# Clustered attention and a feed-forward block: seven block products for eight, and the feed-forward work moved behind the attention

## The chip, the cores and the metric

The kernel runs on one core of a Trainium2 chip. The metric is the device time of one execution in microseconds. The kernel before takes 1087.33 us (median of three runs, 1086.96 to 1087.64).

The core has a matrix engine (TensorE, PE in the profile, with PEld for its weight loads), VectorE (DVE), ScalarE (ACT), GpSimd (POOL) and SyncE (SP), which issues the transfers here.

## What is computed

Attention in which a query sees only the keys of its own cluster, then a feed-forward block without bias:

```python
# q, k, v: (4, 8, 768, 64); centroids: (8, 16, 64)
q_assign = argmax(q_n @ c_n.T);  k_assign = argmax(k_n @ c_n.T)   # of 16 clusters, per head
scores = q @ k.T / sqrt(64), where q_assign == k_assign, else -1e9
attn_out = softmax(scores) @ v                                    # (4, 8, 768, 64)
x = attn_out as (4 * 768, 512)                                    # tokens x (heads * 64)
h = x @ w_in                                                      # (3072, 2048)
g = h * sigmoid(1.702 * h)
out = g @ w_out                                                   # (3072, 512)
```

All matmuls are done in float32. The weights arrive as float64 and are turned into float32 on the chip, early in the run.

## The kernel before

The names: a *pair* is two heads of a batch (16 pairs). A *unit* is one tile of 128 keys against half of the queries (384) of both heads of a pair. Six units make a *group* g. A batch has 8 groups, first four for its first half of queries, then four for the second. The main loop goes through 96 *steps* t of two units each, 24 steps to a batch.

```python
ps_s: 2 score buffers of two PSUM banks each;  ps_o: 1 bank;  ps_m: 3 banks  # bank()

def scores(u):      # TensorE: k^T q of both heads into a score buffer      (L384)
def exps(u):        # ScalarE: exp, in place in the score buffer            (L409)
def mask(u):        # VectorE: A = (code of query == code of key) * exp     (L420)
                    # GpSimd: sum of A over the units of the group          (L430)
def values(u):      # TensorE: o += v^T A                                   (L441)
def normalise(g):
    # TensorE: column sums of `sum` by a matmul with ones, into bank()      (L453)
    rec = recs[g] = short()
    nc.vector.reciprocal(out=rec, in_=ps[:, 0:HALF])                      # (L456)
    nc.vector.tensor_tensor(out=x, in0=x, in1=rec, op=ALU.mult)           # (L458)
    if g % HP == HP - 1:                  # four pairs done: half of a batch
        ffn.extend(ffn_chunks(g // HP))
def check(g):       # is rec within limits?
    nc.scalar.activation(out=rec, in_=rec, func=AF.Copy, accum_out=...)   # (L468)
    nc.scalar.activation(out=rec, in_=rec, func=AF.Relu, ..., accum_out=...)  # (L470)

# ffn_chunks(half of a batch): 16 chunks `first`, then 12 chunks `second`
def first(f):       # 4 matmuls of 384 columns into bank()                  (L487)
    nc.scalar.activation(out=g, in_=ps, func=AF.Tanh, scale=0.851)        # (L492)
    nc.vector.scalar_tensor_tensor(g = (g + 1) * ps)                      # (L494)
def second(n, part):  # 4 matmuls of 512 columns; one bank for 4 chunks     (L504)
    # after the last part: ScalarE halves it to y (L510), transfer to out

# prep of a pair, seven parts: turns i = 0..3 (L262, ScalarE copy L267),
# near (L276), assign (VectorE L293 to L316), spread (transfers)
t = b * TB + (-20, -8, -2, 1)[hp] + i       # step of part i of pair hp of batch b

for t in range(NT + 2):
    scores, exps, mask of units 2t, 2t + 1
    values of the two units before
    normalise(g), if a group ended two steps ago       # from mid-batch 0 on; earlier
    prep parts of this step                            # steps do prep first
    if recs: check(*recs)
    owed += rate; as many chunks of ffn as are owed    # rate = 28 / 11.5 = 2.43
# ... some cuts: the unpacking of weights in batch 0 (`round_next`)
while ffn: ffn.popleft()()                  # what is left at the end
```

So each half of a batch is fed forward while the next half's attention runs.

Of the kernel before, what the change touches and what calls it, by code (L numbers as in the profile page):

```python
# [8 lines left out]
FP32 = mybir.dt.float32  # L9
BF16 = mybir.dt.bfloat16  # L10
I32 = mybir.dt.int32
U32 = mybir.dt.uint32
U8 = mybir.dt.uint8
AF = mybir.ActivationFunctionType
ALU = mybir.AluOpType
AX = mybir.AxisListType
# [22 lines left out]
def fast(  # L39
# [18 lines left out]

    nc = tc.nc

    B, H, S, D = q.shape
    NC = centroids.shape[1]
    DM, DF = moe_w_in.shape
# [8 lines left out]
    SCALE = D ** -0.5  # L74
    LIMIT = float(2 ** 20)
    FAR = float(2 ** 120)
    assert D == 64 and NC == 16 and H * NC == P and NJ == 6 and DM == H * D

    PS = bass.MemoryType.PSUM
    NPB = HP + 1  # L80
    const = ctx.enter_context(tc.tile_pool(name="const", bufs=1))
    inp = ctx.enter_context(tc.tile_pool(name="inp", bufs=3))
    pairs = ctx.enter_context(tc.tile_pool(name="pairs", bufs=NPB))
    wp = ctx.enter_context(tc.tile_pool(name="wp", bufs=3))
    asg = ctx.enter_context(tc.tile_pool(name="asg", bufs=2))
    tmp = ctx.enter_context(tc.tile_pool(name="tmp", bufs=3))
    ap = ctx.enter_context(tc.tile_pool(name="ap", bufs=4))
    xp = ctx.enter_context(tc.tile_pool(name="xp", bufs=HP + 2))
    gp = ctx.enter_context(tc.tile_pool(name="gp", bufs=NF))
    yp = ctx.enter_context(tc.tile_pool(name="yp", bufs=2))  # L90
    dram = ctx.enter_context(tc.tile_pool(
        name="dram", bufs=2, space=bass.MemoryType.DRAM))
    ps_s = ctx.enter_context(tc.tile_pool(name="ps_s", bufs=2, space=PS))
    ps_o = ctx.enter_context(tc.tile_pool(name="ps_o", bufs=1, space=PS))
    ps_m = ctx.enter_context(tc.tile_pool(name="ps_m", bufs=3, space=PS))
    ctx.enter_context(tc.manual_schedule())

    def bank():
        return ps_m.tile([P, 512], FP32, name="m")
# [54 lines left out]
    def split_w(i):  # L154

        hi = w_raw[i][:, :, 1]
        w = w_chunks[i][0]
        e = wp.tile([P, WN], I32, name="e")
        nc.vector.tensor_scalar(out=e, in0=hi, scalar1=EXP, scalar2=None,  # L159
                                op0=ALU.bitwise_and)  # L160
        nc.vector.tensor_scalar(out=w.bitcast(I32), in0=hi, scalar1=0xFFFFF,
                                scalar2=None, op0=ALU.bitwise_and)
        nc.scalar.activation(out=e, in_=e, func=AF.Relu, scale=8.0,  # L163
                             bias=low[:, 0:1])
        nc.scalar.activation(out=w, in_=w.bitcast(I32), func=AF.Copy,
                             scale=2.0 ** -20, bias=1.0)
        w_pow[i] = e
# [14 lines left out]
    def round_next():  # L182
        i = w_done[0]
        if i < NW:
            load_w(i + 2)
            split_w(i)
        if 0 < i <= NW:
            join_w(i - 1)
        w_done[0] += 1
# [25 lines left out]
    rank = const.tile([P, NC], BF16, name="rank")  # L215
    nc.vector.tensor_copy(out=rank, in_=rank_f)

    hot = const.tile([P, NJ * 4, 32], BF16, name="hot")
    nc.vector.memset(hot, 0.0)
    sums = const.tile([P, 2, 2 * NPAIR], FP32, name="sums")  # L220

# [226 lines left out]
    def normalise(g):  # L448

        sm = sum_of.pop(g)  # L450
        ps = bank()
        for a in range(2):
            nc.tensor.matmul(out=ps[a * D:(a + 1) * D, 0:HALF], lhsT=ones,  # L453
                             rhs=sm[:, a, :], start=True, stop=True)
        rec = recs[g] = short()
        nc.vector.reciprocal(out=rec, in_=ps[:, 0:HALF])  # L456
        x = xT_of[g] = O_of.pop(g)
        nc.vector.tensor_tensor(out=x, in0=x, in1=rec, op=ALU.mult)  # L458
        if g % HP == HP - 1:
            ffn.extend(ffn_chunks(g // HP))  # L460

    recs = {}

# [8 lines left out]
                             accum_out=sums[:, 1, g:g + 1])  # L472


    ffn = deque()

    def ffn_chunks(bh):
        b, h = divmod(bh, 2)
        xT = [xT_of.pop(bh * HP + c) for c in range(NCH)]
        hs, ys = {}, {}  # L480

        def first(f):

            round_to((f * P // WN + 1) * NCH)
            ps = bank()
            for c in range(NCH):
                nc.tensor.matmul(out=ps[:, 0:HALF],  # L487
                                 lhsT=w_in[:, c, f * P:(f + 1) * P],
                                 rhs=xT[c], start=(c == 0),
                                 stop=(c == NCH - 1))  # L490
            g = hs[f] = gp.tile([P, HALF], FP32, name="g")
            nc.scalar.activation(out=g, in_=ps[:, 0:HALF], func=AF.Tanh,  # L492
                                 scale=0.851)
            nc.vector.scalar_tensor_tensor(out=g, in0=g, scalar=1.0,  # L494
                                           in1=ps[:, 0:HALF], op0=ALU.add,
                                           op1=ALU.mult)

        def second(n, part):
            round_to(NW // 2 + 4 * (part + 1))
            if part == 0:  # L500
                ys[n] = bank()
            ps = ys[n]
            for f in range(4 * part, 4 * part + 4):
                nc.tensor.matmul(out=ps[:, 0:DM],  # L504
                                 lhsT=hs[f][:, n * P:(n + 1) * P],
                                 rhs=w_out[:, f, :],
                                 start=(f == 0), stop=(f == NF - 1))
            if part == NF // 4 - 1:
                y = yp.tile([P, DM], FP32, name="y")
                nc.scalar.mul(y, ps[:, 0:DM], 0.5)  # L510
                nc.sync.dma_start(
                    out=out[b * S:(b + 1) * S, :].rearrange(
                        "(p j) n -> p j n", j=NJ)[:, h * NH + n, :], in_=y)

        return ([lambda f=f: first(f) for f in range(NF)]
                + [lambda n=n, part=part: second(n, part)
                   for n in range(NH) for part in range(NF // 4)])

# [6 lines left out]
    for p in range(1, NPAIR):  # L527
        b, hp = divmod(p, HP)
        for i in range(2 if p == 1 else 0, len(PREP)):
            if p == 1:  # L530
                t = (i - 2) // 2
            elif b == 0:
                t = (hp - 2) * TG + 1 + i // 2
            else:
                t = b * TB + (-20, -8, -2, 1)[hp] + i
            prep_at.setdefault(t, []).append((p, i))
    loads = deque((p, w) for p in range(NPAIR) for w in range(2))
    for _ in range(3):
# [15 lines left out]
    for t in range(NT + 2):  # L554
        us = range(2 * t, 2 * t + 2) if t < NT else ()
        for u in us:
            scores(u)
        if t == 0:
            prep(0, 6)
        for u in us:  # L560
            part(u)
        for u in us:
            exps(u)
        second = t >= TB // 2
        if second:
            round_next()
        for u in us:
            mask(u)
        work = sorted(prep_at.get(t, ()), key=lambda w: PREP[w[1]] != prep_near)
        while work and PREP[work[0][1]] == prep_near:  # L570
            prep(*work.pop(0))
        if 1 <= t <= NT:
            for u in range(2 * t - 2, 2 * t):
                values(u)
        owed = owed + rate if ffn else 0.0
        g = (t - 2) // TG if t >= 2 and (t - 2) % TG == TG - 1 else None
        if g is not None and second:
            normalise(g)
        for p, i in work:
            prep(p, i)  # L580
        if g is not None and not second:
            normalise(g)
        if recs:
            check(*recs)
        if second or t and t % 4 != 3:
            round_next()
        while owed >= 1 and ffn:
            ffn.popleft()()
            owed -= 1
        if second and t % 2:  # L590
            round_next()


    ok = const.tile([P, 2, 2 * NPAIR], FP32, name="ok")
    nc.vector.tensor_scalar(out=ok, in0=sums, scalar1=LIMIT, scalar2=None,
                            op0=ALU.is_le)
    ok1 = const.tile([P, 1], FP32, name="ok1")
    nc.vector.tensor_reduce(out=ok1, in_=ok, axis=AX.XY, op=ALU.min)
    for _ in range(NF // 2):
        ffn.popleft()()  # L600
    ps = bank()
    nc.tensor.transpose(out=ps[0:1, 0:P], in_=ok1, identity=ident)
    okt = const.tile([1, 1], FP32, name="okt")
    nc.vector.tensor_reduce(out=okt, in_=ps[0:1, 0:P], axis=AX.X, op=ALU.min)
    bad = const.tile([1, 1], I32, name="bad")
    nc.vector.tensor_scalar(out=bad, in0=okt, scalar1=-1.0, scalar2=1.0,
                            op0=ALU.mult, op1=ALU.add)
    while ffn:
        ffn.popleft()()
        if len(ffn) == 4:  # L610
            is_bad = nc.values_load(bad[0:1, 0:1], min_val=0, max_val=1)
    return is_bad


@with_exitstack
def general(
# [436 lines left out]
```

## Time and profile before

| engine | busy us | share |
|---|---|---|
| PE (TensorE) | 1049.0 | 96% |
| DVE (VectorE) | 490.8 | 45% |
| ACT (ScalarE) | 354.8 | 33% |
| POOL (GpSimd) | 296.9 | 27% |

The same by stretches of the run, in us of busy time:

| stretch | PE | DVE | ACT | POOL | granted clock |
|---|---|---|---|---|---|
| 0 to 100 | 80.14 | 71.81 | 53.78 | 46.54 | 0.95 |
| 100 to 190 | 80.53 | 85.75 | 50.21 | 26.03 | 0.94 |
| 190 to 280 | 88.93 | 33.09 | 29.05 | 23.34 | 1.00 |
| 280 to 400 | 120.00 | 50.52 | 35.03 | 34.55 | 1.00 |
| 880 to 1000 | 120.00 | 47.20 | 32.55 | 34.37 | 1.00 |
| 1000 to 1087 | 81.40 | 9.53 | 9.65 | 0.00 | 0.99 |

How to read it: [...] A line of a group gives the source line, the engine and operation, the tile written and those read, the shapes and the count. After the first bar stand the busy time and the mean duration of one in ns, and after the second the idle time of the engine just before, with what ended it. In the timeline, a row is the start in us, the time covered in us, and the instructions merged into it, and in brackets the idle time before. The granted clock is the share of full speed that TensorE was given. Matmuls overlap each other, so their durations add up to more than the time they occupy.

### The profile page before, as it was taken

The numbers are of one execution on the slowest core, as the hardware profiler recorded it, in microseconds if no ns is written. First come the engines' busy times: TensorE is split into PE (matmuls) and PEld (weight loads), VectorE is DVE, ScalarE is ACT, GpSimd is POOL, SyncE is SP. The second block draws the span as 40 slices with busy tenths as digits, with TensorE's granted clock in tenths as the row PEclk, the third lists the DMA queues.
The fourth block names the chain that finished last, engine by engine and source line by source line (L and its number), as shares of the span: only waits on it lengthen the run. The fifth ranks groups of instructions, "written<-read, shape, count | busy, mean of one in ns | idle before, by whom it ended". The sixth has DMA issues, their size and how long they took to land. (4 is left out here: it accounts for less than half of the span.)

```text
span 1087.3 us, 10456 instructions
## 1 busy us (share of the span) xinstructions
PE 1049.0 (96%) x3982; PEld 492.6 (45%) x3982; DVE 490.8 (45%) x744; ACT 354.8 (33%) x665; POOL 296.9 (27%) x168
## 2 busy tenths in 40 slices
PE   7878799999999999999999999999999999999997
PEld 3423344445544455444454445444554445444543
DVE  3889999225442344424453164423552344431200
ACT  3755555223422333223432233223332133311100
POOL 2644223213232333123231142222332333230000
PEclk9998899999999999999999999999999999999999
DMA  7623443110100010002100000010000000000000
GB/s 199 165 81 116 131 133 111 46 49 17 49 23 27 10 30 15 31 25 54 51 23 17 15 20 15 15 48 32 8 7 12 10 10 1 1 10 20 1 11 22
DMA packets 64813, 45.13 MB, mean 42 GB/s; under 512 B 51953, under 2 KB 57585, under 8 KB 64753
## 3 DMA queue, kind: packets, MB, share of 16 engines
q1 hardware_dynamic: 64608, 44.33, 14.3%
q8 instruction: 33, 0.54, 0.2%
q14 instruction: 28, 0.22, 0.1%
q10 hardware_dynamic: 144, 0.03, 0.0%
HBM read 38.04 MB, written 6.31 MB: 41 GB/s over the span
## 5 line engine op out<-in xcount | busy, mean ns | idle before, releaser
L430 POOL TENSOR_TENSOR sum<-sum,A 128x768 f32<-128x768 f32 x128 | 235.5, 1840 | 461.3 <-DVE A L420 364.1
L487 PE MATMUL m<-x,w_in 128*128 128x384 f32 x1024 | 347.1, 494 | 9.7 <-ACT T L267 4.4
L504 PE MATMUL m<-w_out,g 128*128 128x512 f32 x768 | 337.8, 594 | 0.7 <-ACT short L282 0.7
L420 DVE SCALAR_TENSOR_TENSOR A<-qb,code,s 128x384 f32<-128x384 uint8 x288 | 157.6, 609 | 274.6 <-ACT s L409 251.9
L487 PEld LDWEIGHTS m<-x,w_in 128*128 128x128 f32 x1024 | 192.2, 192 | 149.1 <-issue 16.3
L504 PEld LDWEIGHTS m<-w_out,g 128*128 128x128 f32 x768 | 143.3, 190 | 175.6 <-issue 171.5
L494 DVE SCALAR_TENSOR_TENSOR g<-g,m 128x384 f32<-128x384 f32 x128 | 70.0, 553 | 220.4 <-ACT g L492 220.3
L384 PE MATMUL s<-T,T 64*128 64x384 f32 x768 | 152.9, 517 | 9.7 <-ACT A L409 9.6
L409 ACT ACTIVATE s<-s 128x768 f32<-128x768 f32 x144 | 107.9, 792 | 136.0 <-PE s L384 136.0
L441 PE MATMUL o<-A,inv 128*64 128x384 f32 x768 | 146.3, 502 | 0.0
L492 ACT ACTIVATE g<-m 128x384 f32<-128x384 f32 x128 | 61.7, 487 | 196.4 <-PE m L487 196.3
L430 POOL TENSOR_TENSOR sum<-A 128x768 f32<-128x768 f32 x32 | 60.0, 1876 | 215.6 <-DVE A L420 179.5
L384 PEld LDWEIGHTS s<-T,T 64*128 64x128 f32 x768 | 66.6, 189 | 94.6 <-issue 52.2
L456 DVE RECIPROCAL short<-m 128x384 f32<-128x384 f32 x32 | 81.6, 2551 | 25.8 <-PE m L453 25.8
L441 PEld LDWEIGHTS o<-A,inv 128*64 128x64 f32 x768 | 46.8, 137 | 84.8 <-issue 84.1
L510 ACT ACTIVATE y<-m 128x512 f32<-128x512 f32 x24 | 14.3, 595 | 155.8 <-PE m L504 142.7
L468 ACT ACTIVATE short<-short 128x384 f32<-128x384 f32 x32 | 16.7, 523 | 111.2 <-DVE x L458 111.2
L409 ACT ACTIVATE A<-s 128x768 f32<-128x768 f32 x48 | 36.1, 804 | 22.0 <-PE s L398 22.0
L267 ACT COPY T<-m 128x384 f32<-128x384 f32 x64 | 29.7, 480 | 37.2 <-PE m L262 37.1
L262 PE MATMUL m<-ident,in 128*128 128x128 f32 x192 | 33.9, 298 | 3.1 <-ACT T L267 1.7
L163 ACT ACTIVATE e<-e,low 128x512 int32<-128x512 int32 x32 | 23.1, 722 | 28.8 <-DVE e L159 28.8
L262 PEld LDWEIGHTS m<-ident,in 128*128 128x128 f32 x192 | 21.5, 146 | 22.4 <-issue 11.9
(68 smaller groups left out, 373.5 us busy)
## 6 DMA issues: line engine op xcount, KB each, us to landing
raw<-in_moe_w_in_dram SPq DMA_DIRECT2D x16, 512.0 KB
raw<-in_moe_w_out_dram SPq DMA_DIRECT2D x16, 512.0 KB
in<-in_q_dram SPq DMA_DIRECT2D x32, 192.0 KB
in<-in_k_dram SPq DMA_DIRECT2D x32, 192.0 KB
inv<-in_v_dram SPq DMA_DIRECT2D x16, 384.0 KB
out_dram<-y SPq DMA_DIRECT2D x24, 256.0 KB
qb<-line SPq DMA_DIRECT2D x12, 192.0 KB
line<-row SPq DMA_DIRECT2D x12, 1.5 KB
```

What stands on the lines that cost most here:

```text
L262: nc.tensor.transpose(out=ps[:, n * P:(n + 1) * P], in_=qk_in[p, w][:, h * NH + n].rearrange("p a d -> p (a d)"), identity=ident)
L267: nc.scalar.copy(dst, ps[:, 0:HALF])
L384: nc.tensor.matmul(out=ps[:, a, 0:HALF], lhsT=T[p, 1][rows, kt * P:(kt + 1) * P], rhs=T[p, 0][rows, h * HALF:(h + 1) * HALF], start=True, ...
L409: nc.scalar.activation(out=A_of[u] if p < HP else s, in_=s, func=AF.Exp, scale=SCALE)
L420: nc.vector.scalar_tensor_tensor(out=A_of[u][:, a, :], in0=qcode[p][:, a, h * HALF:(h + 1) * HALF], scalar=code[p][:, kt % NH, 1, kt // NH ...
L430: nc.gpsimd.tensor_tensor(out=sum_of[g], in0=A_of[u - 1] if kt == 1 else sum_of[g], in1=A, op=ALU.add)
L441: nc.tensor.matmul(out=o_of[g][a * D:(a + 1) * D, 0:HALF], lhsT=v_in[p][:, a, kt, :], rhs=A[:, a, :], start=(kt == 0), stop=(kt == NJ - 1))
L456: nc.vector.reciprocal(out=rec, in_=ps[:, 0:HALF])
L487: nc.tensor.matmul(out=ps[:, 0:HALF], lhsT=w_in[:, c, f * P:(f + 1) * P], rhs=xT[c], start=(c == 0), stop=(c == NCH - 1))
L492: nc.scalar.activation(out=g, in_=ps[:, 0:HALF], func=AF.Tanh, scale=0.851)
L494: nc.vector.scalar_tensor_tensor(out=g, in0=g, scalar=1.0, in1=ps[:, 0:HALF], op0=ALU.add, op1=ALU.mult)
L504: nc.tensor.matmul(out=ps[:, 0:DM], lhsT=hs[f][:, n * P:(n + 1) * P], rhs=w_out[:, f, :], start=(f == 0), stop=(f == NF - 1))
```

## The change

The first layer of the feed-forward block is h = w_in^T x. Take w_in as 2 x 2 blocks (halves of the 2048 outputs by halves of the 512 inputs), and x as 2 x 2 blocks (halves of the inputs by the two halves of a batch's tokens). This product of blocks takes eight block products. There is a scheme with seven products and fifteen block additions or subtractions (Winograd's form of Strassen's), and the change uses it for batches 1, 2 and 3. For this it needs both halves of a batch's x at once, sums of weight blocks (made once) and sums of x blocks (per batch), and room for them in SBUF, which is there only when the attention's buffers are free. So these three batches are fed forward behind all attention.

The attention of batches 1 to 3 would then have no other matmuls beside it. Batch 0's second half is kept for that: it is cut into 48 small chunks (token tiles of 128: two f of the first layer, or two f of the second), of which 0.62 are done in a step, and the last eight are kept for the moment when the sums are made. Batch 0's first half is fed forward as before, during its second half's attention.

For room, pairs have four buffers, not five, and the preparation of a batch's first pair starts 8 steps ahead, not 20. The three banks of `ps_m` stay. Behind the attention, the score banks and the `o` bank become five banks `ps_b` for the seven products.

The core of the diff (cuts marked ...):

```diff
-    NPB = HP + 1
+    NPB = HP
-    xp = ctx.enter_context(tc.tile_pool(name="xp", bufs=HP + 2))
-    gp = ctx.enter_context(tc.tile_pool(name="gp", bufs=NF))
+    xp = ctx.enter_context(tc.tile_pool(name="xp", bufs=NX))        # NX = 26
+    gp = ctx.enter_context(tc.tile_pool(name="gp", bufs=NF // 4))   # of 512 columns
 ...
+    def ffn_tiles():                       # batch 0, second half
+        def first2(n, i):
+            ps = bank()
+            for f in (2 * i, 2 * i + 1):
+                for c in range(NCH):
+                    nc.tensor.matmul(out=ps[:, f % 2 * P:(f % 2 + 1) * P],
+                                     lhsT=w_in[:, c, f * P:(f + 1) * P],
+                                     rhs=xT[c][:, n * P:(n + 1) * P], ...)
+            ...                             # tanh and gelu of 256 columns
+        def second2(n, i): ...              # two matmuls of 512 columns
 ...
-                t = b * TB + (-20, -8, -2, 1)[hp] + i
+                t = b * TB + (-8, -5, -2, 1)[hp] + i
 ...
-        owed = owed + rate if ffn else 0.0
+        todo = half_ffn or (ffn if len(ffn) > NF // 2 else ())
+        owed += (rate if half_ffn else 0.62) if todo else -owed
 ...
+    ps_b = ctx.enter_context(tc.tile_pool(name="ps_b", bufs=5, space=PS))
+    def sums_w(lo, hi): ...                 # VectorE: 8 sums of weight blocks
+    def sums_x(b): ...                      # VectorE: 8 sums of x blocks
+    def seven(f, X, T, gs):
+        def product(a, x):
+            ps = ps_b.tile([P, 512], FP32, name="b")
+            for c in range(2):
+                nc.tensor.matmul(out=ps[:, 0:HALF], lhsT=a(c), rhs=x(c), ...)
+            return ps[:, 0:HALF]
+        p = product(lambda c: A(0, 0, c, *r), lambda c: X[0, 0, c])
+        nc.scalar.copy(g1[:, 0], p)
+        p = product(lambda c: Sa(2, c, *r), lambda c: T[2, c])
+        add(g2[:, 1], p, g1[:, 0])          # VectorE
+        ...                                 # five more products, six more adds
+        for g in (g2, g1):
+            gelu(g, th.tile([P, 2, HALF], FP32, name="th"), g)
+
+    sums_w(0, 2 * P)
+    XT = sums_x(1)
+    sums_w(2 * P, FB * P)
+    while ffn:
+        ffn.popleft()()                     # the eight chunks left
 ...
+    for b in range(1, B):
+        for f in range(FB):                 # FB = 8
+            seven(f, *XT, gs)
+        for h in range(2):
+            for n in range(NH):
+                if (h, n) == (0, 1) and b < B - 1:
+                    XT = sums_x(b + 1)
+                ...
+                for f in range(NF):
+                    second(2 * b + h, n, f, gs[f][:, h, n * P:(n + 1) * P], ps)
```

More of the change, by code (lines that the diff above doesn't have):

```diff
@@ L76, in fast @@
     FAR = float(2 ** 120)
+    NX = 6 * HP + 2
     assert D == 64 and NC == 16 and H * NC == P and NJ == 6 and DM == H * D
     PS = bass.MemoryType.PSUM
-    NPB = HP + 1
+    NPB = HP
     const = ctx.enter_context(tc.tile_pool(name="const", bufs=1))
[L82 to L87, printed above, removed]
-    xp = ctx.enter_context(tc.tile_pool(name="xp", bufs=HP + 2))
-    gp = ctx.enter_context(tc.tile_pool(name="gp", bufs=NF))
[L90 to L94, printed above, removed]
+    xp = ctx.enter_context(tc.tile_pool(name="xp", bufs=NX))
+    gp = ctx.enter_context(tc.tile_pool(name="gp", bufs=NF // 4))
+    yp = ctx.enter_context(tc.tile_pool(name="yp", bufs=1))
     ps_m = ctx.enter_context(tc.tile_pool(name="ps_m", bufs=3, space=PS))
     ctx.enter_context(tc.manual_schedule())
+    att = ExitStack()
+    inp = att.enter_context(tc.tile_pool(name="inp", bufs=3))
+    pairs = att.enter_context(tc.tile_pool(name="pairs", bufs=NPB))
+    wp = att.enter_context(tc.tile_pool(name="wp", bufs=3))
+    asg = att.enter_context(tc.tile_pool(name="asg", bufs=2))
+    tmp = att.enter_context(tc.tile_pool(name="tmp", bufs=3))
+    ap = att.enter_context(tc.tile_pool(name="ap", bufs=4))
+    hp1 = att.enter_context(tc.tile_pool(name="hp1", bufs=1))
+    dram = att.enter_context(tc.tile_pool(
+        name="dram", bufs=2, space=bass.MemoryType.DRAM))
+    ps_s = att.enter_context(tc.tile_pool(name="ps_s", bufs=2, space=PS))
+    ps_o = att.enter_context(tc.tile_pool(name="ps_o", bufs=1, space=PS))
     def bank():
@@ L157, in split_w @@
         w = w_chunks[i][0]
-        e = wp.tile([P, WN], I32, name="e")
+        e = wp.tile([P, WN], I32, name="e", bufs=2)
         nc.vector.tensor_scalar(out=e, in0=hi, scalar1=EXP, scalar2=None,
@@ L216, in fast @@
     nc.vector.tensor_copy(out=rank, in_=rank_f)
-    hot = const.tile([P, NJ * 4, 32], BF16, name="hot")
+    hot = hp1.tile([P, NJ * 4, 32], BF16, name="hot")
     nc.vector.memset(hot, 0.0)
@@ L458, in normalise @@
         nc.vector.tensor_tensor(out=x, in0=x, in1=rec, op=ALU.mult)
-        if g % HP == HP - 1:
-            ffn.extend(ffn_chunks(g // HP))
+        if g % HP == HP - 1 and g < 2 * HP:
+            (half_ffn, ffn)[g // HP].extend((ffn_half, ffn_tiles)[g // HP]())
     recs = {}
@@ L472, in check, with gelu, second, ffn_half @@
                              accum_out=sums[:, 1, g:g + 1])
[L475 to L480, printed above, removed]
+    def gelu(g, t, h):
+        nc.scalar.activation(out=t, in_=h, func=AF.Tanh, scale=0.851)
+        nc.vector.scalar_tensor_tensor(out=g, in0=t, scalar=1.0, in1=h,
+                                       op0=ALU.add, op1=ALU.mult)
+    def second(bh, n, f, g, ps):
+        nc.tensor.matmul(out=ps[:, 0:DM], lhsT=g, rhs=w_out[:, f, :],
+                         start=(f == 0), stop=(f == NF - 1))
+        if f == NF - 1:
+            b, h = divmod(bh, 2)
+            y = yp.tile([P, DM], FP32, name="y")
+            nc.scalar.mul(y, ps[:, 0:DM], 0.5)
+            nc.sync.dma_start(
+                out=out[b * S:(b + 1) * S, :].rearrange(
+                    "(p j) n -> p j n", j=NJ)[:, h * NH + n, :], in_=y)
+    half_ffn, ffn = deque(), deque()
+    def ffn_half():
+        xT = [xT_of.pop(c) for c in range(NCH)]
+        gs, ys = {}, {}
         def first(f):
@@ L490, in first, with second3 @@
                                  stop=(c == NCH - 1))
[L491 to L498, printed above, removed]
+            g = gs[f] = (xp.tile([P, HALF], FP32, name="x") if f % 4 else
+                         gp.tile([P, 4 * P], FP32, name="g")[:, 0:HALF])
+            gelu(g, g, ps[:, 0:HALF])
+        def second3(n, part):
             round_to(NW // 2 + 4 * (part + 1))
@@ L501, in second, with second2 @@
                 ys[n] = bank()
-            ps = ys[n]
             for f in range(4 * part, 4 * part + 4):
[L504 to L513, printed above, removed]
-        return ([lambda f=f: first(f) for f in range(NF)]
-                + [lambda n=n, part=part: second(n, part)
-                   for n in range(NH) for part in range(NF // 4)])
+                second(0, n, f, (gs.pop(f) if n == NH - 1 else gs[f])[
+                    :, n * P:(n + 1) * P], ys[n])
+        return ([lambda f=f: first(f) for f in range(NF)]
+                + [lambda n=n, q=q: second3(n, q)
+                   for n in range(NH) for q in range(NF // 4)])
+    def ffn_tiles():
+        xT = [xT_of.pop(HP + c) for c in range(NCH)]
+        gs, ys = {}, {}
+        def first2(n, i):
[4 more added lines that the diff above has]
+                                     lhsT=w_in[:, c, f * P:(f + 1) * P],
+                                     rhs=xT[c][:, n * P:(n + 1) * P],
+                                     start=(c == 0), stop=(c == NCH - 1))
+            if i % 2 == 0:
+                gs[i // 2] = gp.tile([P, 4 * P], FP32, name="g")
+            g = gs[i // 2][:, i % 2 * 2 * P:(i % 2 + 1) * 2 * P]
+            gelu(g, g, ps[:, 0:2 * P])
+        def second2(n, i):
+            if i == 0:
+                ys[n] = bank()
+            g = gs[i // 2] if i % 2 == 0 else gs.pop(i // 2)
+            for f in (2 * i, 2 * i + 1):
+                second(1, n, f, g[:, f % 4 * P:(f % 4 + 1) * P], ys[n])
+        return [c for n in range(NH) for c in
+                [lambda n=n, i=i: first2(n, i) for i in range(NF // 2)]
+                + [lambda n=n, i=i: second2(n, i) for i in range(NF // 2)]]
     NT = NU // 2
@@ L563, in fast @@
             exps(u)
-        second = t >= TB // 2
-        if second:
+        second_half = t >= TB // 2
+        if second_half:
             round_next()
@@ L574, in fast @@
                 values(u)
-        owed = owed + rate if ffn else 0.0
+        todo = half_ffn or (ffn if len(ffn) > NF // 2 else ())
+        owed += (rate if half_ffn else 0.62) if todo else -owed
         g = (t - 2) // TG if t >= 2 and (t - 2) % TG == TG - 1 else None
-        if g is not None and second:
+        if g is not None and second_half:
             normalise(g)
@@ L580, in fast @@
             prep(p, i)
-        if g is not None and not second:
+        if g is not None and not second_half:
             normalise(g)
@@ L584, in fast @@
             check(*recs)
-        if second or t and t % 4 != 3:
+        if second_half or t and t % 4 != 3:
             round_next()
-        while owed >= 1 and ffn:
-            ffn.popleft()()
+        while owed >= 1 and todo:
+            todo.popleft()()
             owed -= 1
-        if second and t % 2:
+        if second_half and t % 2:
             round_next()
+    qcode.clear()
+    att.close()
+    FB = NF // 2
+    sp = ctx.enter_context(tc.tile_pool(name="sp", bufs=1))
+    tp = ctx.enter_context(tc.tile_pool(name="tp", bufs=6))
@@ new lines, in fast, with A, Sa @@
+    gb = ctx.enter_context(tc.tile_pool(name="gb", bufs=NF))
+    th = ctx.enter_context(tc.tile_pool(name="th", bufs=1))
+    ps_b = ctx.enter_context(tc.tile_pool(name="ps_b", bufs=5, space=PS))
+    S_of = {(i, c): sp.tile([P, FB * P], FP32, name=f"S{i}{c}")
+            for i in (1, 2, 4) for c in range(2)}
+    def A(row, col, c, lo=0, hi=FB * P):
+        at = row * FB * P
+        return w_in[:, 2 * col + c, at + lo:at + hi]
+    def Sa(i, c, lo, hi):
+        return A(1, 0, c, lo, hi) if i == 3 else S_of[i, c][:, lo:hi]
@@ new lines, in sums_w @@
+    def sums_w(lo, hi):
+        r = (lo, hi)
+        for c in range(2):
+            for o, a, b, op in (
+                    (Sa(1, c, *r), A(1, 0, c, *r), A(1, 1, c, *r), ALU.add),
+                    (Sa(2, c, *r), Sa(1, c, *r), A(0, 0, c, *r), ALU.subtract),
+                    (Sa(4, c, *r), A(0, 1, c, *r), Sa(2, c, *r), ALU.subtract),
+                    (Sa(3, c, *r), A(0, 0, c, *r), A(1, 0, c, *r),
+                     ALU.subtract)):
+                nc.vector.tensor_tensor(out=o, in0=a, in1=b, op=op)
@@ new lines, in sums_x @@
+    def sums_x(b):
+        X = {(r, h, c): xT_of.pop((2 * b + h) * HP + 2 * r + c)
+             for r in range(2) for h in range(2) for c in range(2)}
+        T = {}
+        for c in range(2):
+            T[1, c] = X.pop((0, 1, c))
+            for i in (2, 3, 4):
+                T[i, c] = tp.tile([P, HALF], FP32, name="T")
+            for o, a, b in ((T[3, c], X[1, 1, c], T[1, c]),
+                            (T[1, c], T[1, c], X[0, 0, c]),
+                            (T[2, c], X[1, 1, c], T[1, c]),
+                            (T[4, c], X[1, 0, c], T[2, c])):
+                nc.vector.tensor_tensor(out=o, in0=a, in1=b, op=ALU.subtract)
+        return X, T
@@ new lines, in seven, with add @@
+    def seven(f, X, T, gs):
+        r = (f * P, (f + 1) * P)
+        def product(a, x):
+            ps = ps_b.tile([P, 512], FP32, name="b")
+            for c in range(2):
+                nc.tensor.matmul(out=ps[:, 0:HALF], lhsT=a(c), rhs=x(c),
+                                 start=(c == 0), stop=(c == 1))
+            return ps[:, 0:HALF]
+        def add(o, a, b):
+            nc.vector.tensor_tensor(out=o, in0=a, in1=b, op=ALU.add)
+        g1, g2 = (gb.tile([P, 2, HALF], FP32, name="gb") for _ in range(2))
+        gs[f], gs[f + FB] = g1, g2
+        p = product(lambda c: A(0, 0, c, *r), lambda c: X[0, 0, c])
+        nc.scalar.copy(g1[:, 0], p)
+        p = product(lambda c: Sa(2, c, *r), lambda c: T[2, c])
+        add(g2[:, 1], p, g1[:, 0])
+        p = product(lambda c: Sa(1, c, *r), lambda c: T[1, c])
+        add(g1[:, 1], p, g2[:, 1])
+        p = product(lambda c: Sa(3, c, *r), lambda c: T[3, c])
+        add(g2[:, 0], p, g2[:, 1])
+        add(g2[:, 1], p, g1[:, 1])
+        p = product(lambda c: Sa(4, c, *r), lambda c: X[1, 1, c])
+        add(g1[:, 1], p, g1[:, 1])
+        p = product(lambda c: A(1, 1, c, *r), lambda c: T[4, c])
+        add(g2[:, 0], p, g2[:, 0])
+        p = product(lambda c: A(0, 1, c, *r), lambda c: X[1, 0, c])
+        add(g1[:, 0], p, g1[:, 0])
+        for g in (g2, g1):
+            gelu(g, th.tile([P, 2, HALF], FP32, name="th"), g)
@@ L598, in fast @@
     nc.vector.tensor_reduce(out=ok1, in_=ok, axis=AX.XY, op=ALU.min)
[L599 to L602, printed above, removed]
     okt = const.tile([1, 1], FP32, name="okt")
-    nc.vector.tensor_reduce(out=okt, in_=ps[0:1, 0:P], axis=AX.X, op=ALU.min)
     bad = const.tile([1, 1], I32, name="bad")
[L606 to L611, printed above, removed]
+    for b in range(1, B):
+        gs = {}
+        for f in range(FB):
+            seven(f, *XT, gs)
+        if b == B - 1:
+            ps = bank()
+            nc.tensor.transpose(out=ps[0:1, 0:P], in_=ok1, identity=ident)
+            nc.vector.tensor_reduce(out=okt, in_=ps[0:1, 0:P], axis=AX.X,
+                                    op=ALU.min)
+            nc.vector.tensor_scalar(out=bad, in0=okt, scalar1=-1.0,
+                                    scalar2=1.0, op0=ALU.mult, op1=ALU.add)
+        for h in range(2):
+            for n in range(NH):
+                if (h, n) == (0, 1) and b < B - 1:
+                    XT = sums_x(b + 1)
+                if (b, h, n) == (B - 1, 1, NH - 1):
+                    is_bad = nc.values_load(bad[0:1, 0:1], min_val=0,
+                                            max_val=1)
+                ps = bank()
+                for f in range(NF):
+                    second(2 * b + h, n, f, gs[f][:, h, n * P:(n + 1) * P], ps)
     return is_bad
```

## The prediction

> **What bounds the kernel now.** I read the page's busy line first, then its forty slices, then the groups of instructions, and last the timeline of one stretch.
>
> ```profile
> PE 1049.0 (96%) x3982; PEld 492.6 (45%) x3982; DVE 490.8 (45%) x744; ACT 354.8 (33%) x665; POOL 296.9 (27%) x168
> PE   7878799999999999999999999999999999999997
> PEclk9998899999999999999999999999999999999999
> L487 PE MATMUL m<-x,w_in 128*128 128x384 f32 x1024 | 347.1, 494 | 9.7 <-ACT T L267 4.4
> L504 PE MATMUL m<-w_out,g 128*128 128x512 f32 x768 | 337.8, 594 | 0.7 <-ACT short L282 0.7
> ```
>
> TensorE is the bound. From slice 7 (190 us) to the last but one it is busy all the time, and its two feed-forward groups stand with hardly any idle time before them. Only the first 190 us (weights being unpacked on VectorE) and the last 6 us (the last tile going out) are different. So work taken off TensorE after 190 us shortens the run, unless it uncovers a wait that the feed-forward matmuls hide today. A float32 matmul is two instructions here: 8 halves x 16 x 4 = 512 calls, and the group counts 1024.
>
> The means of the groups (494 and 594 ns) are latencies. The rate comes from rows of the timeline:
>
> ```profile
> 513.31 0.49 PE L262 MATMUL m<-ident,in 128*128 128x128 f32 x3
> 513.64 2.75 PE L487 MATMUL m<-x,w_in 128*128 128x384 f32 x8
> 1074.80 6.60 PE L504 MATMUL m<-w_out,g 128*128 128x512 f32 x15
> ```
>
> Eight matmuls of 384 columns take 2.75 us, of which the last is 0.49, so one starts every (2.75 - 0.49) / 7 = **0.323 us**. For 512 columns it is (6.60 - 0.59) / 14 = **0.429 us**. Three of 128 columns start within 0.33 us: **0.11 us** each. The first L487 also starts 0.11 us after the last of these three[...].
>
> [...] The trace shows a granted clock of 0.95 and 0.94 in the stretches 0 to 100 and 100 to 190 us, where TensorE waits, and 1.00 afterwards. [...]
>
> **Part 1, seven products for eight.** 1024 first-layer instructions become 128 (first half of batch 0) plus 3 x 8 x 7 x 2 x 2 = 672 of 384 columns, plus 3 x 16 x 4 x 2 = 384 of 128 columns. That is 1024 - 800 = 224 fewer at 0.323, or -72.4 us, and 384 more at 0.11, or +41.9. **Net -30.5 us of TensorE.** The small pieces cost nothing extra, since three of them take 0.33 against 0.323. The second layer is unchanged.
>
> The price on VectorE: per f, seven additions at about 0.55 us (L494, same width, 553 ns) and two 768-wide gelus at about 0.96 us (from 692 ns for 512 and 558 for 384 columns, the quickest L177 and L458, both with two SBUF inputs), 5.8 us in all, beside 28 x 0.323 = 9.0 us of TensorE. Hidden. The sums of weights and of x are eight 256-wide (0.42), eight 384-wide (0.56) and eight 768-wide (0.96), 15.5 us. Eight left-over pieces (13.7 us of TensorE) and five banks of products stand beside them. Hidden too.
>
> **Part 2, attention without its filler.** Attention of batches 1 to 3 runs in steps of two units. Steps are numbered 0 to 95 and one starts with L384. Today 2.43 feed-forward chunks fill a step to about 10.4 us. Now there is at most one, in 62 steps of 100, 16 x 0.11 or 4 x 0.43 = 1.73 us. Does anything else hold the step up? Step 61 of the kernel before happens to have no filler, and shows it:
>
> ```profile
> 623.29 1.56 PE L384 MATMUL s<-T,T 64*128 64x384 f32 x8
> 626.13 0.81 PE L453 MATMUL m<-sum,ones 128*64 128x384 f32 x4
> 626.87 1.58 PE L384 MATMUL s<-T,T 64*128 64x384 f32 x8
> ...
> 625.20 2.19 DVE L420 SCALAR_TENSOR_TENSOR A<-qb,code,s 128x384 f32<-128x384 uint8 x4 [11.24 <-ACT s L409]
> 627.31 2.55 DVE L456 RECIPROCAL short<-m 128x384 f32<-128x384 f32 x1
> 629.89 0.71 DVE L458 TENSOR_TENSOR x<-x,short 128x384 f32<-128x384 f32 x1
> ...
> 630.64 0.52 ACT L468 ACTIVATE short<-short 128x384 f32<-128x384 f32 x1 [4.83 <-DVE x L458]
> 631.81 0.19 ACT L470 ACTIVATION_READ_ACCUMULATOR short<-short,top 128x1 f32 x1
> 631.90 1.49 ACT L409 ACTIVATE s<-s 128x768 f32<-128x768 f32 x2
> ```
>
> The scores of step 62 start at 626.87, and their exponentials could follow at about 627.9. They start at 631.90, because ScalarE's queue first has the check (L468, L470), which waits for reciprocal and product on VectorE, which come after the masks of step 61. TensorE did not notice: two chunks lay in step 62.
>
> Let M be the end of the masks in a step with a normalisation, every third one (627.4 here). Exponentials of the next step start at M + 4.5. The first unit's masks end 2.0 later, and only then is its score buffer free (there are two), so the scores of the step after start at **M + 6.6**. Between scores and the end of their masks lie 4.05 us (635.18, 637.10 + 2.19 and alike elsewhere give 4.1). The third step takes TensorE 2.94 us (scores and values) without filler, held to 3.05 by the same buffers, or 4.67 with a chunk. One period of three steps is thus 6.6 + 3.05 + 4.05 = 13.7 or 6.6 + 4.67 + 4.05 = 15.3 us (0.4 more where a small tanh stands behind the check). Where the third step also has an assignment (L293 to L316, 3.04 us on VectorE), it is about 16.0. From the instruction order of the changed kernel, between the masks of steps 28 and 94 there are 9 periods with an assignment and 13 without (3 of them with a chunk in the third step): 9 x 16.0 + 13 x 14.25 = **329 us**. TensorE's own work there is 66 x 2.94 + 22 x 0.75 (normalisations) + about 21 (preparation) + 37 x 1.73 = 296. So **about 33 us of stall** come up.
>
> **The sum.** Scores of step 26 start at 244.2 us, and up to there little changes. Steps 26 to 28 are full: 15.3, so M is 259.5 in step 28. Plus 329 is 589 in step 94; masks of step 95 7.7 later, last sum and normalisation 3.5, left-over pieces 13.7, giving 614. Three batches at 8 x 9.04 + 192 x 0.429 = 154.7 make 464, so 1078; the way out of the last tile is 6 (1081.4 to 1087.3 now): 1084. For PSUM banks I add 5 (three for everything, one held by the running output, one by the reciprocal until M + 2.5, so preparation queues for the last one). **1089 us.**
>
> **The rivals.** *TensorE stays the bound*: then only the 30.5 us count, and the result is 1057. For it: VectorE needs only about 3.9 us per step, TensorE 4.7, and shares of busy time would call this safe. Against it: step 61, where the wait is a chain through two queues, not a full engine. *The chain bounds attention*: 1089, as above. *The clock falls too*: a gap of 2.3 us per period, up to 4 in the last unfilled steps[...]. At a few per cent of 340 us this makes 1095 to 1110. *Late operands*: four pair buffers for five, and preparation of each batch's first pair 8 steps ahead instead of 20. Loads still have four steps (20 us), so I give this little.
>
> **Range and chances.** I hold the chain likely, since it is measured; its size could be off by a third (11 us), banks and clock by as much. Range 1072 to 1107. Faster by over 2% means under 1065.6, which needs nearly all stalls absent: 0.09. Slower means over 1109: 0.10.
>
> **What would show it.** L487's successors: 672 product instructions at 0.323 and 384 small ones at 0.11 (wrong if the small ones take 0.19, +30 us). TensorE idle for about 30 us between 260 and 600, in front of the scores, released by the masks. ScalarE waiting at the check for the product, exponentials 4.5 us behind the masks. Steps in threes of 13.7 to 16 us. TensorE full after 600 us. I am wrong if steps average 4.5 us with no idle time, or if products wait for additions.

## The result, and the profile after

The changed kernel takes 1114.82 us (median of four runs, 1112.37 to 1117.42) against 1087.49: **ratio 1.025, interval 1.023 to 1.028**. It is slower, and outside the predicted range of 1072 to 1107.

The page of the changed kernel, busy line and two rows of the slices:

```profile
PE 1039.0 (93%) x4142; PEld 503.9 (45%) x4142; DVE 603.0 (54%) x912; ACT 359.5 (32%) x649; POOL 295.9 (27%) x168
PE   7878799999899998999897899999999999999997
PEclk9989899999989999999998999999999999999999
```

TensorE is busy 10 us less, and idle for 74 us where it was 38; between 260 and 617 us it is busy for 327.5 of 357. The clock row now has two eights in the middle (slices 12 and 22), where every digit was a nine. The kernel behind the attention looks as it should:

```profile
655.95 1.45 PE L700 MATMUL b<-T,w_in 128*128 128x384 f32 x4
657.24 1.45 PE L700 MATMUL b<-x,S 128*128 128x384 f32 x4
...
655.49 1.22 DVE L705 TENSOR_TENSOR gb<-b,gb 128x384 f32<-128x384 f32 x2
657.44 1.85 DVE L705 TENSOR_TENSOR gb<-b,gb 128x384 f32<-128x384 f32 x3 [0.73 <-PE b L700]
```

These are rows of the timeline of batch 1, TensorE first. A product of four instructions starts every 1.29 us, or 0.323 each, without a break. VectorE adds and then waits for TensorE. So the loss is in the attention. This is the stretch from step 31 to step 33, TensorE, VectorE and ScalarE in turn:

```profile
281.06 1.56 PE L392 MATMUL s<-T,T 64*128 64x384 f32 x8
282.55 1.51 PE L449 MATMUL o<-A,inv 128*64 128x384 f32 x8
283.99 2.05 PE L542 MATMUL m<-x,w_in 128*128 128x128 f32 x16
288.25 2.48 PE L392 MATMUL s<-T,T 64*128 64x384 f32 x8 [2.21 <-DVE A L428]
290.65 2.64 PE L449 MATMUL o<-A,inv 128*64 128x384 f32 x8
...
281.47 2.55 DVE L464 RECIPROCAL short<-m 128x384 f32<-128x384 f32 x1
284.06 0.72 DVE L466 TENSOR_TENSOR x<-x,short 128x384 f32<-128x384 f32 x1
286.96 2.19 DVE L428 SCALAR_TENSOR_TENSOR A<-qb,code,s 128x384 f32<-128x384 uint8 x4 [2.19 <-ACT s L417]
...
284.81 0.52 ACT L476 ACTIVATE short<-short 128x384 f32<-128x384 f32 x1 [3.39 <-DVE x L466]
286.07 1.48 ACT L417 ACTIVATE s<-s 128x768 f32<-128x768 f32 x2
```

The scores of step 32 start at 281.06, and their exponentials only at 286.07, behind the check (L476), which waited 3.39 us for the product. The masks follow at 286.96, and at 288.25 the scores of step 33, after TensorE has stood idle for 2.21 us. This is the predicted chain. The second thing is in the last TensorE row: `values` take 2.64 us where they took 1.51 a step earlier. The granted clock had halved: it is 0.50 from 289.58 to 292.98 us. The same in the table by stretches (columns: stretch, length, busy time and count of PE, PEld, DVE, ACT, POOL, then the granted clock, the share of DMA and GB/s):

```profile
280.00:288.00 8.00, 6.04 (x41) 3.21 (x35) 5.78 (x7) 3.27 (x8) 3.63 (x2) 1.00 0.08 25
288.00:295.20 7.20, 6.82 (x32) 3.29 (x32) 3.76 (x8) 2.07 (x3) 5.43 (x3) 0.76 0.01 2
```

0.24 x 7.2 us are 1.7 us of full clock lost, which is 3.4 us at half rate.

### The profile page after: what moved, and what is told of

It reads as the page before. It is cut to its first block, busy times and chain, and to the rows that moved or that the text cites. A ratio compares the mean times of both kernels' runs of the same rounds, so it can differ in the third digit from the quotient of the medians.

```text
span 1113.0 us, 11101 instructions
## 1 busy us (share of the span) xinstructions
PE 1039.0 (93%) x4142; PEld 503.9 (45%) x4142; DVE 603.0 (54%) x912; ACT 359.5 (32%) x649; POOL 295.9 (27%) x168
## 3 DMA queue, kind: packets, MB, share of 16 engines
q1 hardware_dynamic: 64608, 44.33, 13.9%
## 5 line engine op out<-in xcount | busy, mean ns | idle before, releaser
L491 PE MATMUL m<-w_out,gb 128*128 128x512 f32 x576 | 247.7, 592 | 0.0
L705 DVE TENSOR_TENSOR gb<-b,gb 128x384 f32<-128x384 f32 x168 | 93.4, 557 | 213.8 <-PE b L700 207.2
L491 PEld LDWEIGHTS m<-w_out,gb 128*128 128x128 f32 x576 | 109.4, 190 | 137.1 <-issue 136.6
L392 PEld LDWEIGHTS s<-T,T 64*128 64x128 f32 x768 | 68.0, 195 | 113.5 <-issue 38.3
L700 PE MATMUL b<-x,S 128*128 128x384 f32 x192 | 69.8, 486 | 0.0
L700 PE MATMUL b<-T,w_in 128*128 128x384 f32 x192 | 69.8, 486 | 0.0
L700 PE MATMUL b<-x,w_in 128*128 128x384 f32 x192 | 66.3, 486 | 0.0
L513 PE MATMUL m<-x,w_in 128*128 128x384 f32 x128 | 49.6, 543 | 13.3 <-ACT T L275 4.5
L486 DVE SCALAR_TENSOR_TENSOR gb<-th,gb 128x768 f32<-128x768 f32 x48 | 45.8, 954 | 21.8 <-ACT th L485 21.8
L491 PE MATMUL m<-w_out,g 128*128 128x512 f32 x120 | 56.8, 597 | 0.0
L542 PEld LDWEIGHTS m<-x,w_in 128*128 128x128 f32 x384 | 44.7, 192 | 10.7 <-issue 10.6
L476 ACT ACTIVATE short<-short 128x384 f32<-128x384 f32 x32 | 16.7, 523 | 100.8 <-DVE x L466 100.8
```

The source lines that it names most:

```text
L392: nc.tensor.matmul(out=ps[:, a, 0:HALF], lhsT=T[p, 1][rows, kt * P:(kt + 1) * P], rhs=T[p, 0][rows, h * HALF:(h + 1) * HALF], start=True, ...
L486: nc.vector.scalar_tensor_tensor(out=g, in0=t, scalar=1.0, in1=h, op0=ALU.add, op1=ALU.mult)
L491: nc.tensor.matmul(out=ps[:, 0:DM], lhsT=g, rhs=w_out[:, f, :], start=(f == 0), stop=(f == NF - 1))
L513: nc.tensor.matmul(out=ps[:, 0:HALF], lhsT=w_in[:, c, f * P:(f + 1) * P], rhs=xT[c], start=(c == 0), stop=(c == NCH - 1))
L542: nc.tensor.matmul(out=ps[:, f % 2 * P:(f % 2 + 1) * P], lhsT=w_in[:, c, f * P:(f + 1) * P], rhs=xT[c][:, n * P:(n + 1) * P], start=(c == ...
L700: nc.tensor.matmul(out=ps[:, 0:HALF], lhsT=a(c), rhs=x(c), start=(c == 0), stop=(c == 1))
```

## The experiments

My theory: the order in ScalarE's queue (check ahead of the next exponentials) holds the attention, and its idle gaps halve the clock as well. The rivals: VectorE is the limit, late operands, or seven products that don't pay. A measure used throughout is the time from the scores of step 28 to those of step 94, 22 periods of three steps: **352.7 us** in the changed kernel.

### 1. The check one step later

```diff
         for u in us:
             exps(u)
+        if recs:
+            check(*recs)
 ...
-        if recs:
-            check(*recs)
 ...                                        # and once more behind the loop
```

> The two ScalarE instructions of the check are issued one step later, behind that step's exponentials, so nothing in ScalarE's queue waits for the reciprocal and the product before the exponentials. Chain theory: exponentials after a normalisation start 1.0 us behind their scores instead of up to 5.0, the periods without an assignment shrink by 1 to 2.2 us each (about 25 us in all), and with the gaps in front of the scores the six falls of the granted clock in this stage go too (about 10 us): 1080 us, 1074 to 1092. Rival, VectorE itself is the limit (masks wait for reciprocal and product either way): 1105 or more. Rival, late operands: no change, 1115.

Measured: **1075.8 us** (1073.1 to 1078.0), ratio to the kernel before 0.989 (0.987 to 0.990). Step 28 to step 94 takes 320.0 us, 32.7 less. The same three steps, TensorE, VectorE and ScalarE in turn:

```profile
272.82 1.58 PE L392 MATMUL s<-T,T 64*128 64x384 f32 x8
277.76 1.96 PE L392 MATMUL s<-T,T 64*128 64x384 f32 x8
...
275.85 0.71 DVE L466 TENSOR_TENSOR x<-x,short 128x384 f32<-128x384 f32 x1
276.48 2.18 DVE L428 SCALAR_TENSOR_TENSOR A<-qb,code,s 128x384 f32<-128x384 uint8 x4
...
273.84 1.50 ACT L417 ACTIVATE s<-s 128x768 f32<-128x768 f32 x2 [0.65 <-PE s L392]
276.59 0.52 ACT L476 ACTIVATE short<-short 128x384 f32<-128x384 f32 x1 [1.25 <-DVE x L466]
```

Exponentials now start 1.0 us behind the scores, and the next scores 4.9 us behind these instead of 7.2. The masks still wait for the product on VectorE (276.48), so VectorE's queue holds a small rest; the rival that makes it the limit expected 1105. GpSimd's sums hold masks too, by 14.8 us in the changed kernel and 14.0 here between steps 28 and 94, so what was gained did not come from there. No half-rate stretch is left between step 28 and step 94: the granted clock from 254 to 578 us is 1.00. This version beats both kernels.

### 2. A check of double length

```diff
 ...                                        # extra: a new tile
+        if g >= 2 * HP:                    # from batch 1 on
+            nc.scalar.activation(out=rec, in_=rec, func=AF.Copy, accum_out=extra)
+            nc.scalar.activation(out=rec, in_=rec, func=AF.Copy, accum_out=extra)
```

> From batch 1 on the check has two more ScalarE copies with an accumulator, 0.71 us each, so 1.42 us more behind the product and ahead of the exponentials. Chain theory: 1.4 us more in each of the 13 periods without an assignment and some 0.5 in the 9 with one, 20 to 25 us, and perhaps more falls of the clock: 1133 to 1145 us. Rival, ScalarE is idle two thirds of the time and absorbs it: 1115 to 1118.

Measured: **1152.0 us**, 37 more than the changed kernel and above the expected range. In the trace the second added copy, the accumulator's read and the exponentials follow each other without a gap:

```profile
288.57 0.52 ACT L485 ACTIVATE short<-short 128x384 f32<-128x384 f32 x1
289.00 0.19 ACT L485 ACTIVATION_READ_ACCUMULATOR short<-short 128x1 f32 x1
289.09 1.49 ACT L418 ACTIVATE s<-s 128x768 f32<-128x768 f32 x2
```

(The exponentials are L418 in this kernel.) Step 28 to step 94 takes 388.0 us, 35.3 more, or 1.6 per period. TensorE's clock is at half rate in more places too: the mean granted clock of the run is 0.961, against 0.974 in the changed kernel, and between the two steps 47.8 us pass at half rate instead of 23.5. At the price that experiment 5 finds (9.6 us for 23.5), about 10 of the 35.3 us are clock. That is an estimate; it leaves some 25 us for the chain, or 1.15 of the added 1.42 us per period. ScalarE, idle two thirds of the time, absorbs little of it.

### 3. Only the later preparation, in the kernel before

```diff
-    NPB = HP + 1
+    NPB = HP
 ...
-                t = b * TB + (-20, -8, -2, 1)[hp] + i
+                t = b * TB + (-8, -5, -2, 1)[hp] + i
```

> The kernel before with four pair buffers and the preparation of each batch's first pair 8 steps ahead, nothing else of the change. Theory: this costs little, 1087 to 1092, and any loss lies in batch 0. Rival, late operands: 1097 or more, with waits for transfers in every batch.

Measured: 1095.6 us, ratio 1.0073 (1.0058 to 1.0088). Between theory and rival. By the starts of the scores, 3.9 us are lost by step 28, of which 3.0 are won back by step 36, and two losses of some 4 us come in the steps around 45 to 50 and 69 to 74, of which the steps behind win back most of the first. The steps from 18 to 26, beside the moved preparation of batch 1's first pair, take 104.2 us instead of 96.8. I had called this part nearly free.

### 4. Eight plain products behind the attention

The sums of weights and of x and the additions are left out. Each half-batch block is four accumulated matmuls, and the gelu reads PSUM.

```diff
-            seven(f, *XT, gs)
+            eight(f, *XT, gs)              # 32 matmul instructions, not 28
```

> The changed kernel with the plain eight block products behind the attention: no sums of weights or x, no additions, the gelu reads PSUM. 96 more matmul instructions of 384 columns at 0.323 us. Theory (products run at full rate, additions hidden): 31 us longer than the changed kernel, 1146, 1141 to 1150. Rival, additions and banks cost the seven products a part of their gain: 1120 to 1138.

Measured: **1144.7 us**, 29.8 more than with seven. The attention is the same program in both and differs by a few us between traces, so the stretch behind it is the sharper measure: from the scores of step 94 to the end it is 530.6 us against 499.6. The scheme brings the whole of 96 x 0.323 = 31 us; additions and banks take next to nothing of it.

### 5. TensorE kept busy in the gaps

```diff
+        if t in (32, 35, 38, 56, 59, 80, 89, 92):
+            ps = bank()
+            for _ in range(8):             # read by nobody
+                nc.tensor.matmul(out=ps[:, 0:P], lhsT=ident, rhs=ident, start=True, stop=True)
```

> The changed kernel with eight useless matmuls of 128 columns (16 instructions, about 1.8 us) at the end of steps 32, 35, 38, 56, 59, 80, 89 and 92, where TensorE stands idle for 2.1 to 4.2 us in front of the scores. They lengthen nothing if the chain through the check is what holds the scores. If the falls of the granted clock in the steps behind these gaps (six, 1.2 to 2.3 us each) come from the idle time, they go: 10 us less than the changed kernel, 1105, 1101 to 1109. Rival, the clock falls for another reason or costs nothing: 1113 to 1117. Rival, TensorE is the bound after all: 1125 or more.

Measured: **1102.5 us** (1100.5 to 1105.1), 12.3 less than the changed kernel, by adding useless work. Timeline of TensorE around the same gap, and the stretch behind it:

```profile
281.30 1.95 PE L638 MATMUL m<-ident 128*128 128x128 f32 x16
283.65 1.97 PE L392 MATMUL s<-T,T 64*128 64x384 f32 x8 [0.40 <-DVE A L428]
285.54 1.51 PE L449 MATMUL o<-A,inv 128*64 128x384 f32 x8
...
283.40:290.60 7.20, 6.82 (x42) 3.84 (x44) 4.10 (x9) 3.08 (x5) 5.43 (x3) 1.00 0.01 2
```

Of the gap, 0.40 us is left, and the scores still come 7.2 us behind those of the step before, so the chain is unchanged. The clock stays at 1.00, and `values` take 1.51 us, not 2.64. Step 28 to step 94 takes 343.1 us, 9.6 less, and all of it in the six periods in which the clock had fallen; the other 16 are as long as before to within 0.1 us. So this is what the six falls of the clock cost there. The rest of the 12.3 us is not shown to come from the edit: in its profile, step 28 starts 4.6 us earlier than in the changed kernel's, ahead of the first useless matmul.

### 6. The late check in the kernel before

The edit of the first experiment, in the kernel before.

> The kernel before with the check issued behind the next step's exponentials, the same edit as in the first experiment. Theory: there the wait lies beside feed-forward matmuls, so it costs nothing and nothing is won: 1085 to 1089. Rival, the early check costs time whatever lies beside it: 1070 or less.

Measured: 1087.6 us, ratio 1.000 (0.999 to 1.001). ScalarE's wait for the product ahead of the check shrinks from 111.2 to 3.8 us in all, and nothing is won: the wait costs nothing while feed-forward matmuls lie beside it.

### 7. The check left out

From the last group of batch 0 on nothing is checked (the changed kernel otherwise).

```diff
 ...                                        # sums are set to zero; rec is kept for g < 7 alone
-        if recs:
+        if recs and t < TB:
             check(*recs)
```

> The changed kernel with the check left out for the groups of batches 1 to 3 and the last of batch 0 (its sums are zero there). Theory: the order was the cost and not the check's own 1.4 us of ScalarE per group, so this is as long as the version with the late check: 1076, 1070 to 1080. Rival, ScalarE's own time counts: 1060 to 1068.

Measured: 1079.8 us (1076.9 to 1081.3); step 28 to step 94 takes 321.5 us, as with the late check (320.0). So the order was the cost, not ScalarE's 1.4 us.

### 8. The later preparation with all five buffers

The third experiment with `NPB = HP + 1` as before.

> The kernel before with the later preparation alone (5 pair buffers as before), against the third experiment, which also had one buffer fewer and was 7.8 us slower. If the later preparation itself is the cost (it falls into steps 16 to 22 of batch 0 and beside the next pair's preparation in every batch): 1093 to 1097. If the missing buffer is (preparation waits for a buffer to come free): 1086 to 1090.

Measured: 1094.3 us, ratio 1.0066 (1.0051 to 1.0080). The missing buffer costs little if anything; the later time does. Why preparing later costs 7 us in the kernel before was not followed further.

## Why the prediction failed

The mechanism came true; **the step that failed is the sum**. Three of its terms were too small: "up to there little changes" (by 5.0 us), the length of the 22 periods (by 9), and the clock (9.6), which stood among the rivals and not in the sum.

**Part 1 held**: product instructions at 0.323 us, small ones at 0.112, additions hidden, 29.8 us against 30.5 predicted (the plain version's small pieces are the same, so the 31 is the fair comparison). From the masks of step 94 to the end of the profiled run there are 495 us, predicted 1084 - 589 = 495.

**Part 2, the chain, held in kind**: exponentials at M + 4.5 (masks of step 31 end at 281.56, exponentials at 286.07), the scores of the step after at M + 6.7 against 6.6. TensorE is idle for 29.5 us between 260 and 617 us, as was put.

**The sum failed**, by 26 us. Taken apart on the profiled run (1113.0 us, 24 over the sum; the timed runs are 1.8 us longer than their profile's span):

- "Up to there little changes": the scores of step 26 start at 249.2 us, not at 244.2. **+5.0 us**, nearly all behind step 18 (147.5 against 147.4). From step 18 to step 26 it takes 101.6 us instead of 96.8, and 104.2 in the third and eighth experiments, where the moved preparation is the one edit that both share. So this is the likely cause. Ahead of step 18 the executions differ: the traces of the changed kernel and its variants reach it at 143.0 to 148.0 us, and in the late-check version step 26 starts at 242.6.
- The 22 periods, 329 us and 5 for banks: measured from masks to masks 353, **+19 us**. The fifth experiment gives **9.6** of these to the clock. That was written down as a rival, at "1095 to 1110", and left out of the middle and of the range. It should have been a term of the sum: the gap of 2.3 us per period had been worked out in the same text.
- The other 9 lie in the periods themselves. With a steady clock (fifth experiment), the 9 with an assignment take 151.3 us where 144 were put, and the 13 without take 191.8 where 185.25 were put, 13.9 more in all, of which the 5 for banks were in the sum. In the 13, most of it is the third step: it takes 5.32 us with a chunk where 4.67 were put (start of step 57 at 420.78, of step 58 at 426.10), and 3.34 without, where 3.05 were put. Sixteen small instructions take 2.0 us until the next scores, not 1.73: they start 0.112 us apart, and 0.2 passes behind the last. And the scores of the third step take 1.90 us until the values, not 1.49, because the second unit's wait for their buffer, a wait that I had seen and taken as covered.
- Six of the 9 (from steps 43, 46, 49, 67, 70 and 73) are not held by the chain, as "about 16.0" assumed: they take 101.9 us together with the early check at a steady clock and with the late one. This is the one from step 46, in the changed kernel and in the late-check version, where TensorE is busy for 16.2 of 17.1 us either way:

```profile
359.31:376.41 17.10, 16.19 (x85) 6.92 (x84) 12.47 (x20) 8.77 (x17) 8.97 (x6) 1.00 0.32 81
339.92:357.03 17.11, 16.20 (x86) 6.92 (x85) 12.57 (x20) 8.74 (x17) 9.07 (x6) 1.00 0.36 82
```

Put in the prediction's own two parts: it had 296 us of TensorE's own work and 33 of stall. With the chain broken the stretch takes 320.0 us (TensorE busy for 311.2), and the chain adds 23.1 to that.

**The rivals**: *late operands* are a side cost of a few us, and not through waits for transfers (such waits are 1.7 us in all at the most, in any of these runs). *TensorE stays the bound* said 1057; with the chain broken it is 1075.8. *The clock falls too* came true beside the chain.

The account of the loss: the seven products bring 30 us. Taking the feed-forward work away from the attention uncovers a chain that costs 23.1 us between steps 28 and 94 (343.1 with a steady clock against 320.0), and 9.6 us of clock on top. These 32.7 are shown; the late-check version is 39 us faster. Of the rest, its profile has 2.5 us behind step 94 and 6.6 ahead of step 28 (254.1 against 260.7), but 4.4 of these come ahead of step 18, where traces with the early check differ by as much.

The late-check version is 12 us below the kernel before and not 30. In its profile, 16.0 below, TensorE is busy for 29.5 us less (1019.5 against 1049.0), as the seven products give, and idle for 13.5 us more (51.8 against 38.3): about 3.7 of these ahead of step 28, 6.7 from there to step 94, and 3.2 behind. The later preparation (7 us in the kernel before) is probably a part of them; how much stays open.

The idle time that ScalarE spends ahead of the check, waiting for the product, in the changed kernel and in the late-check version (total in us, number of times):

```profile
  DVE x L466: 100.8, 32
...
  DVE x L466: 17.4, 12
```

Before the change it was 111.2 us, 32 times, and cost nothing (experiment 6).

## What to carry to other kernels

Before moving filler away from a pipelined loop, find the slack it covers: look for an iteration of the old trace that has no filler, and follow there which queue holds the next iteration's first instruction. Bookkeeping that waits for a slow result belongs, in the order of issue, behind the next iteration's urgent work: here the exponentials, issued behind the check, started 5.0 us behind their scores, while ScalarE stood idle for 3.39 us ahead of the check. The move took 32.7 us off 22 periods, while the same move in the kernel before, where other work covered the wait, was worth nothing (ratio 1.000). And where idle gaps of TensorE are foreseen, count the clock that they cost (9.6 us of 352.7 here) in the sum itself.

## What the runs showed of the hardware

Behind idle gaps of 2.07 to 2.26 us TensorE's granted clock fell to 0.50 for 3.4 us (289.58 to 292.98 behind the gap of 2.21 us in front of step 33), though not each time: of the gaps in front of steps 33, 36, 39, 57, 60 and 81 of the changed kernel, the clock fell behind four, and behind those of 57 and 60 (2.07 and 2.19 us) it did not. In the trace of the fourth experiment, whose attention is the same program, it fell behind these two as well (2.07 and 2.20 us). The stretch from step 57 on, there and in the changed kernel:

```profile
417.30:424.50 7.20, 7.04 (x34) 3.74 (x36) 3.53 (x7) 2.23 (x4) 5.43 (x3) 0.76 0.00 1
420.78:427.98 7.20, 7.06 (x44) 3.88 (x46) 3.86 (x8) 3.32 (x6) 5.44 (x3) 1.00 0.00 1
```

Which of two gaps of the same length the clock falls behind, and why, was not shown. Of the six falls between steps 28 and 94, five lasted 3.4 us and one 6.8 (607.02 to 613.82 us, beside a gap of 4.18 us in front of step 93). Filling the gaps with useless matmuls removed all six (mean granted clock of the run 0.985, against 0.974).
